# Four banks for attention, a three-step weight decode and ScalarE softmax steps in the first twelve slots of a fused attention and feed-forward kernel

## The chip, the cores and the metric

The kernel runs on one core of a Trainium2 chip. The metric is the device time of one execution in microseconds (us), and the median of several runs is quoted. Five engines work side by side, each through its own queue in order: PE (TensorE, matmuls), DVE (VectorE), ACT (ScalarE), POOL (GpSimd) and SP (SyncE, which here issues every DMA). An instruction that waits holds up everything behind it on its engine.

## What is computed

Attention over keys and values that are mean-pooled by eight, then two feed-forward layers, all in float32. Shapes: batch 8, 8 heads, 576 tokens, head size 64, so 72 pooled keys a head; then 4608 tokens by 512, with 2048 hidden units in each layer.

```python
def _attn_ref(q, k, v):
    k_p = k.reshape(B, H, Sp, pool, D).mean(axis=3)      # 576 keys -> 72
    v_p = v.reshape(B, H, Sp, pool, D).mean(axis=3)
    scores = scale * np.matmul(q, k_p.transpose(0, 1, 3, 2))
    scores = scores - np.max(scores, axis=-1, keepdims=True)
    attn = np.exp(scores)
    attn = attn / (np.sum(attn, axis=-1, keepdims=True) + 1e-09)
    return np.matmul(attn, v_p)

def _moe_ref(x, w_in, w_out):
    h = x @ w_in
    return (h * np.clip(h + 3.0, 0.0, 6.0) / 6.0) @ w_out

def _moe2_ref(x, w_in, w_out, a, b):
    h = x @ w_in
    P = a[0] + a[1] * h + a[2] * h**2 + a[3] * h**3
    Q = 1.0 + np.abs(b[0]) * np.abs(h) + np.abs(b[1]) * h**2
    return (P / (Q + 1e-6)) @ w_out
```

## The kernel before

Every large product is made from two parts of each operand: a rounded high part and the remainder as a low part, both in a faster float32 form. High by high, high by low and low by high give three matmuls per block. So each weight chunk and each activation is split by ScalarE (the rounding copy) and VectorE or GpSimd (the subtraction).

**Slots.** The program is a list of slots, written out in order by `slot(s)`. Nothing reorders it afterwards. Slots -12 to -1 (`PRE = 12`) are a start-up; from slot 0 on, each slot of layer 1 holds one hidden block (`hidden`, line 448, twelve matmuls into `ps_h`) and one output block of two slots ago (`out1`, line 473, into `ps_y`). Layer 1 has 9 token blocks of 16 slots, then layer 2 has as many. What a slot holds besides is put into lists by kind (`el`, `pe`, `ex`, `nz`, `mid`, `hi`, `la`, and `dm` and `ld` for loads), and `slot` goes through these lists in a fixed order, the same before slot 0 as after.

**Attention.** A unit is 128 (or fewer) query tokens for four heads. Its steps are: `scores` (line 334, PE), `highest` (the maximum, line 349, and its scaling, line 350, both DVE), `exponentials` (line 359, four ACT instructions that also give the sums), `normalize` (line 368 adds 1e-9 to the sums and line 370 takes the reciprocal, both DVE; lines 371 and 377 multiply on POOL), `transposes` (line 386, three on PE), `split_p` (line 397 on ACT, lines 398 and 402 on DVE). After the units of one half of the heads, `attend` (line 415, eight matmuls) multiplies by the values, and `split_x` (lines 426 and 427) makes the layer's input. The transposes of unit i and the scores of unit i+2 stand in one slot, the exponentials and the normalizing of unit i+1 in the same slot. In slots -10 to -1 stand the transposes t0 to t3, an attend (slot -6), t4 to t7, and an attend (slot -1): ten slots for eight units and two attends. Scores, transposes and attends take turns on two PSUM banks, `a0` and `a1`:

```python
    def bank_a(name):
        turn[0] ^= 1
        return ps_a.tile([P, 512], F32, tag=f"a{turn[0]}", name=name)
```

**The first values.** For batch 0 the pooling of the values is done on PE: `pool_first_v` (line 279) makes eight small matmuls per chunk, six chunks in all, three in slot -11 and three in slot -10. `split_v` (line 293 on ACT, 294 on DVE), `mask_v` (line 303, POOL) and `mask_rest` (lines 314 to 319, DVE) make the operands of the attend from them, in slots -10 and -9.

**Weights.** Layer 1 has 32 chunks of 128x512. They come as raw 64-bit words and are turned into float32 by `decode_a` and `decode_r` (lines 153 and 158, ACT), `decode_b` (lines 172 and 173, DVE) and `decode_c` (line 180, POOL), then split by `split_weights` (line 200 ACT, 202 DVE or POOL). In the start-up, chunk i is decoded in slot i-12 and split one slot later (chunks 10 and 11 both in slot -2, chunk 12 in slot -1), all by `make_ready`, which stands in the list `el`: behind the exponentials of the slot and ahead of its normalizing, its `split_p` and its maximum.

Of the kernel before, what the change touches and what calls it, by code (L numbers as in the profile page):

```python
# [68 lines left out]
def feed_forward_kernel(tc, q_t, k_t, v_r, vmask, w_in1, w_out1, w_in2, w_out2, a_rep, b_rep, out):  # L69
# [25 lines left out]
    def consts():  # L95
# [8 lines left out]
        nc.gpsimd.memset(cst[:, 1:2], (1.0 + 1e-6) * 2.0 ** -LN_SHIFT)  # L104
        nc.gpsimd.memset(cst[:, 2:3], -LN_SHIFT * math.log(2.0))
        nc.vector.tensor_scalar(
            out=coef[:, 6:10], in0=coef[:, 0:4], scalar1=-1.0, scalar2=None, op0=ALU.mult
# [41 lines left out]
    def decode_a(*c):  # L149
        hi = raw[c].bitcast(I32).rearrange("p (n t) -> p n t", t=2)[:, :, 1].bitcast(F32)  # L150

        dec[c] = ps_h.tile([P, DM], F32, tag="h", name="d") if c[0] == 0 and 2 * c[1] + c[2] < PRE else hi
        nc.scalar.activation(out=dec[c], in_=hi, func=AF.Copy, scale=2.0 ** -112)
# [170 lines left out]

    def bank_a(name):
        turn[0] ^= 1
        return ps_a.tile([P, 512], F32, tag=f"a{turn[0]}", name=name)

    def scores(b, g, f, ti):
        _, n = ti  # L330
        ps = bank_a("ps_s")
        q = q_sb.pop((b, f, ti))
        for i in range(2):
            nc.tensor.matmul(  # L334
                ps[:n, i * 2 * SP:(i + 1) * 2 * SP],
                lhsT=q[:, i, :n],
                rhs=kbd[:, 2 * f + i].rearrange("p j s -> p (j s)"),
                start=True,
                stop=True,
            )  # L340
        sc_ps[b, f, ti] = ps
# [3 lines left out]
    def highest(b, f, ti):  # L345
# [3 lines left out]
        nc.vector.tensor_reduce(out=nm[:n], in_=ps, axis=AX.X, op=ALU.max, negate=True)  # L349
        nc.vector.tensor_scalar(out=nm[:n], in0=nm[:n], scalar1=SCALE, scalar2=None, op0=ALU.mult)  # L350

    def exponentials(b, f, ti):
        _, n = ti
        ps, nm = sc_ps.pop((b, f, ti)), s_max.pop((b, f, ti))
        s = s_sb[b, f, ti] = att.tile([P, 2 * PK + P], F32, tag="s", bufs=2, name="s")
        sm = s_sum[b, f, ti] = att.tile([P, 4], F32, tag="sm", bufs=2, name="sm")
        for h in range(4):
            c = slice(h * SP, (h + 1) * SP)
            nc.scalar.activation(  # L359
                out=s[:n, c], in_=ps[:n, c], func=AF.Exp, scale=SCALE, bias=nm[:n, h:h + 1], accum_out=sm[:n, h:h + 1]  # L360
            )

    def normalize(b, f, ti):
# [3 lines left out]
        sm = s_sum.pop((b, f, ti))  # L367
        nc.vector.tensor_scalar(out=sm[:n], in0=sm[:n], scalar1=1e-9, scalar2=None, op0=ALU.add)
        rc = att.tile([P, 4], F32, tag="rc", bufs=2, name="rc")
# [11 lines left out]
    def transposes(b, g, f, ti):  # L381
        _, n = ti
        s = s_sb.pop((b, f, ti))
        ps = bank_a("ps_t")
        for c, o in enumerate((0, PK, 2 * PK)):
# [20 lines left out]
    def attend(b, g, f, i):  # L406
        n = GROUPS[b][g][1]
        ph, pl = pth[b, g, f], ptl[b, g, f]
        ps = bank_a("ps_v")
        wh, wl, wr = (  # L410
# [156 lines left out]

    pe, ex, el, nz, mid, hi, la, dm, ld = {}, {}, {}, {}, {}, {}, {}, {}, {}

# [7 lines left out]
    def prepare_first(s0, units):  # L577
# [9 lines left out]
        for c in range(VCH):  # L587
            at(dm, s0, load_v, 0, c)
            at(pe, s0 + 1 + c // 3, pool_first_v, c)
        at(dm, s0, load_weights, 0, *chunks[1])  # L590
        for p in (0, NPAIR, 1):
            at(el, s0, pool_first_k, p)
        for p in (2, 3):
            at(el, s0 + 1, pool_first_k, p)
        at(la, s0 + 2, split_v, 0)
        for i in range(4):
            at(la, s0 + 3 + i // 2, mask_v, 0, i // 2, i % 2)
        at(la, s0 + 3, mask_rest, 0)

# [72 lines left out]
    for i in range(len(chunks) + 1):  # L672
        s = i - PRE if i < 10 else 3 * (i - 10) // 4 - 2
        if 2 <= i < len(chunks):
            at(dm if i < 24 else ld, s - 2, load_weights, 0, *chunks[i])
# [40 lines left out]
    def slot(s):  # L716
        d = s - LAG
        for f in dm.get(s, ()):
            f()
# [105 lines left out]
```

## Time and profile before

| what | us |
|---|---|
| median of 3 runs | 1797.69 |
| lowest and highest of them | 1795.35 and 1800.09 |
| the profiled execution | 1796.08 |
| its span in the profile | 1794.3 |
| PE busy | 1733.5 (97%) |
| DVE busy | 1019.1 (57%) |
| ACT busy | 955.5 (53%) |
| POOL busy | 915.0 (51%) |

PE works nearly all the time over the whole span, and the other engines about half of it. Those shares are means over stages that differ much, so they say little about the first twelve slots, which end where the first matmul into `ps_h` starts, 93.26 us into the span. How to read the views: a timeline row has the start, the time of the row, the engine, the line, the operation, what is written and read, and in brackets how long the engine had been idle and what ended that. Where a row stands for several instructions, its time is that of all of them. A wait is put down to what came last.

### The profile page before, as it was taken

To read this page: it belongs to the slowest core of one execution; us is meant where nothing else is said; L and a number is where in the kernel's file an instruction comes from. 1 tells how busy PE (TensorE), PEld (TensorE's weight loads), DVE (VectorE), ACT (ScalarE), POOL (GpSimd) and SP (SyncE) were. 2 spreads that over 40 slices of the span, in tenths; PEclk is the share of its full clock that TensorE was granted. 3 is DMA by queue.
4 is the path that set the end of the run, shared out by engine and by line. 5 is a ranking of instruction groups with operands and counts; after the bars stand their busy time and mean duration, and the time that the engine had idled before them with its cause. 6 is when DMAs were issued, how large, how long until landed. Compare 5 with 4: busy or idle time off the path is not lost.

```text
span 1794.3 us, 22345 instructions
## 1 busy us (share of the span) xinstructions
PE 1733.5 (97%) x7872; PEld 1433.5 (80%) x7872; DVE 1019.1 (57%) x1771; ACT 955.5 (53%) x2072; POOL 915.0 (51%) x887
## 2 busy tenths in 40 slices
PE   7388999999999999999999999999999999999999
PEld 6276788888888888888888888888888888888887
DVE  4786544646455463643311466666666666666665
ACT  3565444554444454544322466666666666666665
POOL 2556433343434343343323476667666666666665
PEclk9589999999999999999999999999999999999999
DMA  5352122314142242422026401010101010101000
GB/s 175 117 184 83 44 81 67 130 64 161 57 136 91 75 149 64 135 81 80 30 95 220 143 18 36 12 36 13 36 12 41 7 42 6 42 6 42 1 24 24
DMA packets 68336, 128.33 MB, mean 72 GB/s; under 512 B 11392, under 2 KB 27776, under 8 KB 68224
## 3 DMA queue, kind: packets, MB, share of 16 engines
q1 hardware_dynamic: 68224, 126.91, 21.3%
q8 instruction: 62, 1.02, 0.2%
q14 instruction: 50, 0.41, 0.1%
HBM read 91.23 MB, written 35.65 MB: 71 GB/s over the span
## 4 chain that ended last, share of the span: by engine, by line
PE 87%; DVE 1%; ACT 0%; DMA 0%; POOL 0%; issue 0%; SPq 0%; ACTq 0%; DVEq 0%
PE ps_h L448 41%; PE ps_o L553 22%; PE ps_y L473 20%; PE ps_s L334 2%; PE ps_v L415 2%; PE ps_t L386 1%; DMA v_raw<-v_r 0%; ACT s L359 0%; DVE t L173 0%; POOL gl L462 0%; POOL gl L539 0%; ACT y L479 0%; DVE vsum L247 0%; DVE t L172 0%; DVE nm L349 0%
## 5 line engine op out<-in xcount | busy, mean ns | idle before, releaser
L462 POOL TENSOR_TENSOR gl<-r,gh 128x512 fp32r<-128x512 f32 x144 | 187.5, 1302 | 478.5 <-ACT gh L461 474.8
L473 PE MATMUL ps_y<-gh,w 128*128 128x512 f32 x1152 | 391.8, 401 | 0.0
L448 PE MATMUL ps_h<-xh,w 128*128 128x512 f32 x1152 | 379.4, 390 | 0.5 <-DVE r L455 0.5
L448 PE MATMUL ps_h<-x2h,w 128*128 128x512 f32 x1152 | 377.8, 389 | 0.8 <-DVE t L515 0.8
L553 PE MATMUL ps_o<-w,gh 128*128 128x512 f32 x1152 | 354.6, 389 | 0.0
L473 PEld LDWEIGHTS ps_y<-gh,w 128*128 128x128 f32 x1152 | 219.2, 190 | 47.3 <-issue 1.8
L448 PEld LDWEIGHTS ps_h<-xh,w 128*128 128x128 f32 x1152 | 216.8, 188 | 46.2 <-DVE r L455 0.9
L448 PEld LDWEIGHTS ps_h<-x2h,w 128*128 128x128 f32 x1152 | 216.4, 188 | 46.2 <-DVE t L515 1.2
L553 PEld LDWEIGHTS ps_o<-w,gh 128*128 128x128 f32 x1152 | 216.3, 188 | 45.0
L510 POOL TENSOR_SCALAR qd<-ah,coef 128x512 f32<-128x512 f32 x144 | 111.4, 773 | 234.0 <-ACT ah L508 234.0
L473 PE MATMUL ps_y<-gl,w 128*128 128x512 f32 x576 | 226.9, 394 | 0.0
L448 PE MATMUL ps_h<-xl,w 128*128 128x512 f32 x576 | 224.5, 390 | 0.0
L523 DVE SCALAR_TENSOR_TENSOR qd<-qd,r 128x512 f32<-128x512 f32 x144 | 99.0, 688 | 220.5 <-ACT r L522 204.0
L448 PE MATMUL ps_h<-x2l,w 128*128 128x512 f32 x576 | 224.1, 389 | 0.0
L553 PE MATMUL ps_o<-w,gl 128*128 128x512 f32 x576 | 224.1, 389 | 0.0
L539 POOL TENSOR_TENSOR gl<-g,gh 128x512 fp32r<-128x512 f32 x144 | 186.5, 1295 | 19.3 <-ACT gh L538 19.3
L513 POOL TENSOR_TENSOR qd<-qd,ah 128x512 f32<-128x512 f32 x144 | 187.1, 1300 | 12.1
L455 DVE SCALAR_TENSOR_TENSOR r<-r,ps_h 128x512 f32<-128x512 f32 x144 | 98.2, 682 | 149.1 <-ACT r L454 148.6
L508 ACT ACTIVATE ah<-ps_h 128x512 f32<-128x512 f32 x144 | 86.1, 598 | 151.9 <-PE ps_h L448 151.9
L521 ACT ACTIVATE r<-qd,cst 128x512 f32<-128x512 f32 x144 | 99.6, 692 | 105.4 <-POOL qd L513 105.4
L461 ACT ACTIVATE gh<-r 128x512 fp32r<-128x512 f32 x144 | 91.3, 634 | 118.7 <-PE ps_y L473 109.2
L359 ACT ACTIVATE s<-ps_s,nm 128x72 f32<-128x72 f32 (+1 forms) x320 | 98.2, 318 | 91.6 <-DVE nm L350 84.8
(89 smaller groups left out, 2608.2 us busy)
## 6 DMA issues: line engine op xcount, KB each, us to landing
raw<-w_in SPq DMA_DIRECT2D x32, 512.0 KB, 3.7
raw<-w_out SPq DMA_DIRECT2D x32, 512.0 KB, 3.8
w<-raw SPq DMA_DIRECT2D x32, 512.0 KB, 2.9
w<-w SPq DMA_DIRECT2D x32, 512.0 KB, 4.1
v_raw<-v_r SPq DMA_DIRECT2D x47, 256.0 KB, 4.0
y<-y SPq DMA_DIRECT2D x36, 256.0 KB, 2.9
x2r<-y SPq DMA_DIRECT2D x36, 256.0 KB, 2.9
out<-o SPq DMA_DIRECT2D x36, 256.0 KB, 2.2
```

What stands on the lines that cost most here:

```text
L359: nc.scalar.activation(out=s[:n, c], in_=ps[:n, c], func=AF.Exp, scale=SCALE, bias=nm[:n, h:h + 1], accum_out=sm[:n, h:h + 1])
L448: nc.tensor.matmul(ps, lhsT=w, rhs=x, start=o == 0, stop=o == len(ops) - 1)
L455: nc.vector.scalar_tensor_tensor(out=r, in0=r, scalar=1.0, in1=ps, op0=ALU.min, op1=ALU.mult)
L461: nc.scalar.activation(out=gh[it], in_=r, func=AF.Copy)
L462: nc.gpsimd.tensor_tensor(out=gl[it], in0=r, in1=gh[it].bitcast(F32), op=ALU.subtract)
L473: nc.tensor.matmul(yp[j][c], lhsT=w, rhs=x, start=m == 0 and o == 0, stop=m == MF - 1 and o == 2)
L510: nc.gpsimd.tensor_scalar(out=qd, in0=ah, scalar1=absb[1], scalar2=absb[0], op0=ALU.mult, op1=ALU.add)
L513: nc.gpsimd.tensor_tensor(out=qd, in0=qd, in1=ah, op=ALU.mult)
L521: nc.scalar.activation(out=r0, in_=qd, func=AF.Ln, scale=2.0 ** -LN_SHIFT, bias=cst[:, 1:2])
L523: nc.vector.scalar_tensor_tensor(out=qd, in0=qd, scalar=1.0 + 1e-6, in1=r0, op0=ALU.add, op1=ALU.mult)
L539: nc.gpsimd.tensor_tensor(out=gl[it], in0=g, in1=gh[it].bitcast(F32), op=ALU.subtract)
L553: nc.tensor.matmul(yp[j][c], lhsT=w, rhs=x, start=m == 0 and o == 0, stop=m == MF - 1 and o == 2)
```

## The change

There are four edits.

- **Banks.** For batch 0's first group (`b + g == 0`) scores, transposes and attends go round four banks: `a0`, `y2`, `a1`, `y3`. The two `y` banks belong to `out1`, which first uses them in slot 2. Later units still alternate between `a0` and `a1`.
- **The order within slots -12 to -1.** These slots get an order of their own: loads, the early `el`, `pe`, the maximum (`hi`), exponentials, normalizing, the middle step of a weight chunk (`c1`), `mid`, the split of the chunk before (`c2`), the first step of the chunk after (`c3`), `la`. The decode of a chunk thus spreads over three slots. Chunks 0 to 10 go this way (before, chunks 0 to 12 were begun by slot -1); from chunk 11 on, three chunks are made ready in two slots, where it was four in three. Both ways reach chunk 24 in slot 8, and chunk 31 in slot 13.
- **Values.** One chunk is summed in slot -11, two in slot -10, two in slot -9, one in slot -8. Splitting and masking move with them by two slots, to slots -8, -7 and -6.
- **Small softmax steps.** The scaling of the maximum and the adding of 1e-9 become ACT instructions on 128x4 elements, in `exponentials`, for all 80 units. DVE loses both.

```diff
-        dec[c] = ps_h.tile([P, DM], F32, tag="h", name="d") if c[0] == 0 and 2 * c[1] + c[2] < PRE else hi
+        dec[c] = ps_h.tile([P, DM], F32, tag="h", name="d") if c[0] == 0 and 2 * c[1] + c[2] < PRE - 1 else hi
...
-    def bank_a(name):
-        turn[0] ^= 1
+    def bank_a(name, first):
+
+        if first:
+            turn[0] = (turn[0] + 1) % 4
+            pool, tag = ((ps_a, "a0"), (ps_y, "y2"), (ps_a, "a1"), (ps_y, "y3"))[turn[0]]
+            return pool.tile([P, 512], F32, tag=tag, name=name)
+        turn[0] = turn[0] % 2 ^ 1
         return ps_a.tile([P, 512], F32, tag=f"a{turn[0]}", name=name)
...
         nc.vector.tensor_reduce(out=nm[:n], in_=ps, axis=AX.X, op=ALU.max, negate=True)
-        nc.vector.tensor_scalar(out=nm[:n], in0=nm[:n], scalar1=SCALE, scalar2=None, op0=ALU.mult)
...
+        nc.scalar.activation(out=nm[:n], in_=nm[:n], func=AF.Copy, scale=SCALE)
         for h in range(4):
...
+        nc.scalar.activation(out=sm[:n], in_=sm[:n], func=AF.Identity, bias=cst[:n, 3:4])
...
-        nc.vector.tensor_scalar(out=sm[:n], in0=sm[:n], scalar1=1e-9, scalar2=None, op0=ALU.add)
...
-            at(pe, s0 + 1 + c // 3, pool_first_v, c)
+            at(pe, s0 + 1 + (c + 1) // 2, pool_first_v, c)
...
-        at(la, s0 + 2, split_v, 0)
+        at(la, s0 + 4, split_v, 0)
         for i in range(4):
-            at(la, s0 + 3 + i // 2, mask_v, 0, i // 2, i % 2)
-        at(la, s0 + 3, mask_rest, 0)
+            at(la, s0 + 5 + i // 2, mask_v, 0, i // 2, i % 2)
+        at(la, s0 + 5, mask_rest, 0)
...
     for i in range(len(chunks) + 1):
-        s = i - PRE if i < 10 else 3 * (i - 10) // 4 - 2
-        if 2 <= i < len(chunks):
+        if i < PRE - 1:
+
+            s, c = i + 1 - PRE, (0, *chunks[i])
+            if i > 1:
+                at(dm, max(s - 3, -PRE), load_weights, *c)
+            at(c3, s - 1, decode_a, *c)
+            at(c3, s - 1, decode_r, *c)
+            at(c1, s, decode_b, *c)
+            at(c1, s, decode_c, *c)
+            if i < PRE - 2:
+                at(c2, s + 1, split_weights, *c)
+            continue
+        s = 2 * (i + 1 - PRE) // 3
+        if i < len(chunks):
             at(dm if i < 24 else ld, s - 2, load_weights, 0, *chunks[i])
         at(el, s, make_ready, i)
...
         d = s - LAG
+        if s < 0:
+            for kind in (dm, ld, el, pe, hi, ex, nz, c1, mid, c2, c3, la):
+                for f in kind.get(s, ()):
+                    f()
+            return
```

On PE the instructions of the first slots stand in this order before (`ps_k` pools the keys, `ps_s` are scores, `ps_vs` the sums of the values, `ps_t` the transposes; x8, x16 and x24 are one, two and three chunks of values).

```order
L334 MATMUL ps_s<-kbd,q_sb 128x144 x2
L279 MATMUL ps_vs<-k_raw,ident 128x64 x8
L279 MATMUL ps_vs<-v_raw,ident 128x64 x16
L386 MATMUL ps_t<-ident,s 128x128 x3
L334 MATMUL ps_s<-kbd,q_sb 128x144 x2
L279 MATMUL ps_vs<-v_raw,ident 128x64 x24
L386 MATMUL ps_t<-ident,s 128x128 x3
L334 MATMUL ps_s<-kbd,q_sb 128x144 x2
```

And after, in the same stretch of PE, up to the fourth set of transposes:

```order
L340 MATMUL ps_s<-kbd,q_sb 128x144 x2
L280 MATMUL ps_vs<-k_raw,ident 128x64 x8
L392 MATMUL ps_t<-ident,s 128x128 x3
L340 MATMUL ps_s<-kbd,q_sb 128x144 x2
L280 MATMUL ps_vs<-v_raw,ident 128x64 x16
L392 MATMUL ps_t<-ident,s 128x128 x3
L340 MATMUL ps_s<-kbd,q_sb 128x144 x2
L280 MATMUL ps_vs<-v_raw,ident 128x64 x16
L392 MATMUL ps_t<-ident,s 128x128 x3
L340 MATMUL ps_s<-kbd,q_sb 128x144 x2
L280 MATMUL ps_vs<-v_raw,ident 128x64 x8
L392 MATMUL ps_t<-ident,s 128x128 x3
```

The first transposes stand behind one chunk of values instead of three, and the other chunks are spread behind the next three units. From there on PE's order is the same in both kernels.

On DVE one start-up slot reads like this before (`t<-d` and `t<-d,t` are decode_b, `w` is the split, `sm` and `rc` belong to normalizing, `ptl` and `pth` to split_p, `nm` to the maximum).

```order
L172 TENSOR_SCALAR t<-d 128x512
L173 SCALAR_TENSOR_TENSOR t<-d,t 128x512
L202 TENSOR_TENSOR w<-t,w 128x512
L368 TENSOR_SCALAR sm<-sm 128x4
L370 RECIPROCAL rc<-sm 128x4
L398 TENSOR_TENSOR ptl<-ps_t,pth 128x2x128
L402 TENSOR_TENSOR pth<-ps_t,pth 32x128
L349 TENSOR_REDUCE nm<-ps_s 128x4
L350 TENSOR_SCALAR nm<-nm 128x4
```

And one start-up slot of DVE after:

```order
L355 TENSOR_REDUCE nm<-ps_s 128x4
L376 RECIPROCAL rc<-sm 128x4
L173 TENSOR_SCALAR t<-d 128x512
L174 SCALAR_TENSOR_TENSOR t<-d,t 128x512
L404 TENSOR_TENSOR ptl<-ps_t,pth 128x2x128
L408 TENSOR_TENSOR pth<-ps_t,pth 32x128
L203 TENSOR_TENSOR w<-t,w 128x512
```

The maximum has moved from the end of the slot to its head, the reciprocal ahead of the decode, and `sm` and the second `nm` are gone.

On ACT one start-up slot after has its two new rows (lines 362 and 368) around the exponentials, and the decode's first step behind everything else:

```order
L362 ACTIVATE nm<-nm 128x4
L365 ACTIVATE s,sm<-ps_s,nm 128x72 x4
L368 ACTIVATE sm<-sm,cst 128x4
L403 ACTIVATE pth<-ps_t 128x3x128
L201 ACTIVATE w<-t 128x512
L154 ACTIVATE d<-raw_260 128x512
L159 ACTIVATE raw_260<-raw_260 128x512
```

Before, lines 153, 158 and 200 stood between the exponentials and the copy into `pth`; now they stand behind it. SP's order is unchanged up to the load of chunk 10: the loads of keys, values, queries and these chunks stand where they stood.

## Rows read from the trace of the kernel before

**Rows 1.** Windows: us, busy us (instructions) of PE, PEld, DVE, ACT, POOL; clock, DMA, GB/s.

```profile
0.00:93.26 93.26, 52.20 (x224) 44.52 (x225) 54.90 (x107) 41.69 (x138) 34.04 (x48) 0.74 0.43 143
93.26:225.00 131.74, 117.23 (x516) 93.92 (x515) 94.78 (x173) 74.38 (x204) 74.30 (x71) 0.93 0.32 104
225.00:900.00 675.00, 674.11 (x3212) 558.81 (x3211) 330.06 (x731) 317.18 (x915) 257.46 (x282) 1.00 0.28 93
```

**Rows 2.** PE's three longest waits, 38 to 93.2 us: total, times, longest.

```profile
PE ps_v L415 <- DVE pth L402: 8.8, 2, 5.7
PE ps_t L386 <- POOL s L377: 8.7, 2, 4.4
PE ps_t L386 <- DVE nm L350: 7.6, 2, 4.0
```

**Rows 3.** Timeline of PE: values, transposes and attends of the start-up, first hidden block.

```profile
24.18 7.03 PE L279 MATMUL ps_vs<-v_raw,ident 128*128 128x64 f32 x32
31.01 0.85 PE L386 MATMUL ps_t<-ident,s 128*128 128x128 f32 x3
...
32.61 6.02 PE L279 MATMUL ps_vs<-v_raw,ident 128*128 128x64 f32 x48
...
52.82 0.90 PE L386 MATMUL ps_t<-ident,s 128*128 128x128 f32 x3 [4.38 <-POOL s L377]
...
57.82 0.76 PE L415 MATMUL ps_v<-pth,vh 128*128 128x512 f32 x1 [3.14 <-DVE pth L402]
...
89.36 0.77 PE L415 MATMUL ps_v<-pth,vh 128*128 128x512 f32 x1 [5.68 <-DVE pth L402]
...
93.26 0.63 PE L448 MATMUL ps_h<-xh,w 128*128 128x512 f32 x1
```

**Rows 4.** Timeline of PE: transposes, then scores, then `ps_y`, later at full clock.

```profile
125.09 0.49 PE L386 MATMUL ps_t<-ident,s 128*128 128x128 f32 x3
...
125.82 0.48 PE L473 MATMUL ps_y<-gh,w 128*128 128x512 f32 x1
```

**Rows 5.** Timeline of ACT in slot -7: exponentials, decode, split, split_p.

```profile
51.80 0.32 ACT L359 ACTIVATE s<-ps_s,nm 128x72 f32<-128x72 f32 x1 [2.75 <-DVE nm L350]
...
53.00 0.64 ACT L153 ACTIVATE d<-raw 128x512 f32<-128x512 f32 x1
...
54.63 0.49 ACT L397 ACTIVATE pth<-ps_t 128x384 fp32r<-128x384 f32 x1
```

**Rows 6.** Timeline of DVE in slot -7: decode, reciprocal, split_p, maximum.

```profile
53.68 0.69 DVE L172 TENSOR_SCALAR t<-d 128x512 int32<-128x512 int32 x1 [1.99 <-ACT d L153]
...
56.89 0.18 DVE L370 RECIPROCAL rc<-sm 128x4 f32<-128x4 f32 x1
56.98 0.39 DVE L398 TENSOR_TENSOR ptl<-ps_t,pth 128x256 fp32r<-128x256 f32 x1
...
57.70 0.46 DVE L349 TENSOR_REDUCE nm<-ps_s 128x4 f32<-128x288 f32 x1
```

**Rows 7.** Timeline of POOL, slots -8 and -7: decode_c, masks, normalizing.

```profile
49.16 1.28 POOL L180 TENSOR_TENSOR t<-t,raw 128x512 int32<-128x512 int32 x1 [2.42 <-ACT pth L397]
...
52.72 0.61 POOL L303 TENSOR_TENSOR vh<-vsh,mask 128x256 fp32r<-128x256 f32 x1
...
57.21 0.40 POOL L371 TENSOR_TENSOR s<-s,rc 128x128 f32<-128x128 f32 x1 [0.38 <-DVE rc L370]
57.69 0.67 POOL L377 TENSOR_TENSOR s<-s,rc 128x288 f32<-128x288 f32 x1
```

**Rows 8.** Groups by line and shape, 0 to 93.3 us: count, busy us, mean ns, idle.

```profile
L368 DVE TENSOR_SCALAR sm<-sm 128x4 f32<-128x4 f32 x8 | 7.8, 976 | 0.0
...
L109 ACT ACTIVATE coef<-coef 128x2 f32<-128x2 f32 x1 | 0.2, 203 | 1.4 <-DMA coef<-b_rep 1.4
```

**Rows 9.** Timeline of POOL and PE in a later slot of layer 1.

```profile
404.06 1.29 POOL L462 TENSOR_TENSOR gl<-r,gh 128x512 fp32r<-128x512 f32 x1 [4.11 <-ACT gh L461]
...
407.26 0.39 PE L473 MATMUL ps_y<-gl,w 128*128 128x512 f32 x1
```

More of the change, by code (lines that the diff above doesn't have):

```diff
@@ L105, in consts @@
         nc.gpsimd.memset(cst[:, 2:3], -LN_SHIFT * math.log(2.0))
+        nc.gpsimd.memset(cst[:, 3:4], 1e-9)
         nc.vector.tensor_scalar(
@@ L330, in scores @@
         _, n = ti
-        ps = bank_a("ps_s")
+        ps = bank_a("ps_s", b + g == 0)
         q = q_sb.pop((b, f, ti))
@@ L383, in transposes @@
         s = s_sb.pop((b, f, ti))
-        ps = bank_a("ps_t")
+        ps = bank_a("ps_t", b + g == 0)
         for c, o in enumerate((0, PK, 2 * PK)):
@@ L408, in attend @@
         ph, pl = pth[b, g, f], ptl[b, g, f]
-        ps = bank_a("ps_v")
+        ps = bank_a("ps_v", b + g == 0)
         wh, wl, wr = (
@@ L565, in evac2 @@
             nc.sync.dma_start(out=out[r:r + P, :], in_=o)
-    pe, ex, el, nz, mid, hi, la, dm, ld = {}, {}, {}, {}, {}, {}, {}, {}, {}
+    pe, ex, el, nz, mid, hi, la, dm, ld, c1, c2, c3 = ({} for _ in range(12))
     def at(kind, slot, f, *a):
```

## The prediction

> **What bounds the kernel now.** I read the windows first, because they say where a change to the start-up can count at all. From 225 to 900 us PE is busy for 674.11 of 675.00 us [rows 1]: there only PE's own work sets the time, and this change leaves that work as it is. Up to 93.26 us PE is busy for 52.20 us, and from there to 225 us for 117.23 of 131.74 us. So 41 us of PE time stand idle before the first hidden block and 14.5 us in the stretch behind it. Whatever brings the first hidden block forward shortens the run by as much, as long as the stretch behind it doesn't hand it back.
>
> The timeline splits the start-up in two. Up to the end of the values PE is full: two chunks take 24.18 to 31.01, then t0 and the next scores until 32.61, then three chunks in 6.02 us [rows 3]. After that the slots wait for a round trip. PE's longest waits are for DVE's `pth` and `nm` and POOL's `s` [rows 2], the ends of each slot's chain: exponentials on ACT, decode and reciprocal on DVE, normalizing on POOL, then DVE's split_p and maximum, from which ACT's next exponentials start. ACT stood idle 2.75 us for `nm` at 51.80, while DVE's decode of 53.68 had waited for ACT [rows 5, 6]. The two take turns, and each slot pays for both in a row.
>
> **The change part by part.** I replay the start-up with durations of rows, PE's marks first. Transposes and scores of a slot take 32.61 - 31.01 = 1.60 us here and 125.82 - 125.09 = 0.73 us later at the higher clock [rows 3, 4]. A chunk of values takes 6.83 / 2 = 3.4 us in the first pair and 6.02 / 3 = 2.0 us in the last three.
>
> *Values.* t0 stands behind one chunk instead of three, so it comes two chunks sooner: 31.0 - 6.8 = 24.2. The other five chunks now lie between the units, and PE is the bound: t0 and scores 1.6, two chunks 6.8 (32.6), t1 and scores 0.73, two chunks 4.0 (37.3), t2 and scores 0.73, the last chunk 2.0: 40.1 for t3. The loop must keep up. Behind the scores that end at 38.1, the maximum takes 0.46, the reciprocal's hand-over to POOL 0.32 (56.89 to 57.21) and normalizing 1.15 (57.21 to 58.36) [rows 6, 7]: 40.0, just in time. So t3 starts at 40.1 instead of 52.82 [rows 3]: 12.7 us won.
>
> *Masks, the part that costs.* They come two slots later and now the first attend waits for them. The high part of the sums takes ACT 0.5 (as the copy at 54.63), to 40.6; `nm`, exponentials (51.80 to 53.00, 1.2) and `sm` 1.6, to 42.2; hand-over and normalizing 1.5, to 43.7 [rows 5, 7]. Then POOL has a decode_c and a split, which with one normalizing took 52.72 - 49.16 = 3.56, so 2.4 without it, to 46.1, and two masks of 0.6 each [rows 7]. The attend's first matmul can go at 46.7 and its third at 47.3; I take 47.0. Before, it was 57.82: 10.8 of the 12.7 are left.
>
> *The four banks and the new order,* slots -6 to -1. An attend lasts 93.26 - 89.36 = 3.9 [rows 3], to 50.9; ACT stands behind it with its copy of the result. t4, t5 and their scores no longer wait, since their inputs were normalized slots earlier and their banks are free. ACT then has one copy of 0.5, twice the group decode and split (53.00 to 54.63, 1.63) and one `pth` of 0.5: 55.2. The softmax of unit 6 takes 1.6, hand-over and normalizing 1.5: t6 at 58.3. For t7, ACT goes on from 56.8 with `pth` 0.5, decode and split 1.63 and unit 7's exponentials with `nm` 1.4, to 60.3. The scores of unit 8 are the first that go back to two banks, and wait for those exponentials: 1.0 for them (1.60 less 0.6 of transposes) and 0.46 for the maximum give 61.8, and behind it on DVE stand the reciprocal 0.1, the decode 2 x 0.69 and split_p 0.72 (56.98 to 57.70) [rows 6]: t7, whose bank split_p frees, at 64.0. Once more with unit 9's scores behind t7 (0.6 + 1.0) and its maximum, 66.1, and the same 2.2 on DVE: the second attend at 68.3 instead of 89.36, the first hidden block at 72.2 instead of 93.26 [rows 3]. That is 21 us. The replay leaves out the small gaps between engines; I take 2 us off for these, an estimate of 4% of the 48 us behind t0. **19 us** remain. The ends: nothing at all if the slots keep their old pace, and 41 us if PE never waited [rows 1].
>
> *Small steps.* In these slots DVE's `sm` took 976 ns on average over 8, far more than the reciprocal's 180 ns; POOL was at its decode_c beside it. An ACT instruction on two columns took 203 ns [rows 8]. I take 0.2 each for the two steps that move. The bounds are 0.1 (hidden in part behind the one ahead) and 0.32, what a 72-column exponential takes [rows 5]: with eight units, 2 us either way, inside the range.
>
> The Trainium skill speaks against this part: its page ScalarE: Activation LUTs, section Rules for kernel authors, puts multiplications and additions on VectorE; by the figures there an ACTIVATE of four columns with a pointer bias would take about 280 ns, an estimate which makes the sum less than 1 us worse. In these slots the trace disagrees with the rule: DVE's 976 ns is the dearer one.
>
> *Slots from 0 on.* DVE loses both steps for the units in the idle stretch up to 225 us, some dozen, and there two more chunks are to be decoded and split, 2 x (2 x 0.69 + 0.7) = 4.2 us of DVE. DVE's 94.78 us of 131.74 [rows 1] become lighter by some 8 us. PE's 14.5 idle us there may shrink or, where two chunks fall into one slot more often, grow. I take 1 us won, with -5 and +4 as ends. In the rest of layer 1, 70 units carry two more ACT steps; 1.9 us lie between POOL's end of `gl` (404.06 + 1.29) and its use at 407.26 [rows 9], so 0.4 us are covered, and without that cover would cost up to 70 x 0.4 = 28 us. Loads keep their order on SP; 143 GB/s [rows 1] become 143 x 93.26 / 72 = 185 for the same bytes, and each load still stands two slots ahead of its use.
>
> Sum against the profiled execution: 1796.08 - 19 - 1 = 1776.1. The median of the runs lies 1.6 above that execution: 1777.7, so **1778 us**.
>
> **The rivals.**
>
> *The slots stay long.* The values' 12.7 us come, the masks take 1.9 back, and behind the first attend the slots keep their old 31.5 us (57.82 to 89.36) because ACT and DVE are still in series, the last two units on two banks: 1797.7 - 10.8 = 1787. For it: five of the waits above pass through ACT, which is held by each attend. Against it: DVE's maximum now goes to the head of the slot, and ACT's idle 2.75 us [rows 5] were the wait for it.
>
> *PE keeps its higher clock.* The granted clock averages 0.74 before 93.26 us [rows 1]. If the tighter slots hold it high, transposes and scores of t0 and t4 to t7 cost 0.87 less each, 4 us, the first two chunks 2.8, the attends about 3.5 together: 10 us more, 1768. Against it: PE would still wait for about a third of slots -7 to -1.
>
> *Slower.* The two steps on ACT cost what `sm` costs on DVE. Then `gh` behind them in each later unit comes late, `gl` too, and PE waits at `ps_y` (line 473). It decides from the 1.9 us of cover [rows 9]: with 1.1 us per step, (2.2 - 1.9) x 70 = 21 us eat the whole gain; at 1.25 per step it is (2.5 - 1.9) x 70 - 20 = +22: 1820. Against it: 203 ns [rows 8]. The skill's rule above is this rival's rule, though its figure is far below that point.
>
> *No change.* The idle time moves behind the first hidden block: the weights or keys of slots 0 to 8 are late on DVE, which is busy 94.78 of 131.74 us there [rows 1], and PE waits there for what it saved: 1797.
>
> **How the numbers follow.** Forecast 0.64, slots stay long 0.20, higher clock 0.08, no change 0.05, slower 0.03. The range goes from 1768, the higher clock, to 1789, which takes in the long slots with 2 us of ACT steps at the upper bound; what is left out is the last two cases and a little of the edges. A measurement of this kernel can tell about 0.3% (5 us) from no change: faster 0.92, same 0.05, slower 0.03.
>
> **What would show it.** t0 near 24, t3 near 40, the first attend near 47 with POOL's masks as its releaser, the first hidden block near 72; no `nm` wait of PE's transposes; ACT's two steps at about 0.2 us; PE full again from about 205. The forecast is wrong if the slots behind the first attend take over 5.5 us, or if PE's idle time behind the first hidden block grows beyond 19 us.

## The result, and the profile after

The changed kernel takes 1776.84 us (median of four runs, 1774.42 to 1780.08), and the kernel before, beside it, 1798.89: a ratio of 0.988 with a 95% interval of 0.986 to 0.991. The profiled execution took 1774.73 us with a span of 1772.9. I call the two kernels "before" and "after".

The first part of the page of after gives busy time, share and instructions:

```profile
PE 1726.1 (97%) x7872; PEld 1429.6 (81%) x7872; DVE 984.0 (56%) x1611; ACT 992.5 (56%) x2232; POOL 911.1 (51%) x888
```

DVE lost 35 us and ACT gained 37, as the small steps moved over; neither bounds the whole. The windows say where the time went (columns as in [rows 1]). They end at the first hidden block, at the point where PE has become full, and inside layer 1:

```profile
0.00:68.59 68.59, 44.15 (x224) 39.65 (x225) 41.64 (x81) 42.53 (x151) 29.48 (x48) 0.81 0.52 176
68.59:203.15 134.56, 117.52 (x515) 94.32 (x513) 95.30 (x156) 83.01 (x231) 77.05 (x72) 0.92 0.34 111
203.15:878.00 674.85, 673.87 (x3211) 558.67 (x3211) 306.94 (x613) 344.97 (x1034) 256.07 (x283) 1.00 0.28 93
```

The start-up fell from 93.26 us to 68.59, and PE's idle time in it from 41.1 to 24.4 us. The stretch behind it became longer: the same work of PE (515 and 516 matmul records) now stands in 134.56 us instead of 131.74, with 17.0 us idle instead of 14.5. The third row is as before [rows 1]: 1 us idle in 675. The clock column counts time for which the trace holds no clock record as 1.00, so the 0.81 here and the 0.74 of [rows 1] are too high (see the last section). On PE's timeline the marks of the forecast read:

```profile
24.75 3.91 PE L280 MATMUL ps_vs<-v_raw,ident 128*128 128x64 f32 x32
...
35.75 0.55 PE L392 MATMUL ps_t<-ident,s 128*128 128x128 f32 x3 [0.19 <-POOL s L383]
...
43.03 0.80 PE L421 MATMUL ps_v<-pth,vh 128*128 128x512 f32 x1 [6.24 <-POOL vh L304]
...
65.04 0.77 PE L421 MATMUL ps_v<-pth,vh 128*128 128x512 f32 x1 [2.77 <-ACT sm L368]
...
68.59 0.63 PE L454 MATMUL ps_h<-xh,w 128*128 128x512 f32 x1
...
233.87 0.48 PE L479 MATMUL ps_y<-gh,w 128*128 128x512 f32 x1
```

The last row is the first matmul of the 21st output block. I use it as a mark behind the stretch in which PE still waits. In before it stands at 255.41:

```profile
255.41 0.48 PE L473 MATMUL ps_y<-gh,w 128*128 128x512 f32 x1
```

From it to the end of the span lie 1539.0 us in after and 1538.9 in before, and between 1538.0 and 1539.3 in every kernel below. So all that differs lies ahead of the mark, and the 57 units behind it (80 less ten in the start-up and thirteen from there to the mark) carry their two more ACT steps for nothing.

PE's waits from 30 us to the first hidden block (total, times, longest) are no longer those of [rows 2]:

```profile
PE ps_v L421 <- POOL vh L304: 6.2, 1, 6.2
PE ps_t L392 <- DVE t L174: 4.8, 1, 4.8
PE ps_v L421 <- ACT sm L368: 2.8, 1, 2.8
PE ps_t L392 <- DVE pth L408: 2.6, 1, 2.6
```

No transposes wait for `nm` any more. The longest wait is the new one, for POOL's masks.

The times of one kernel fall into two groups: after's ten runs gave 1774.0 to 1775.6 or 1778.9 to 1783.5, and before's 1794.8 to 1796.4 or 1797.7 to 1801.4. One difference between executions can be seen in the traces: PE's first pair of value chunks took 3.9 us in the profile above and 6.9 in others, because PE's clock rose later there (last section). So between kernels I compare stretches that begin behind that pair, and give its length:

| kernel | median us | ratio to before (95%) | first value pair | t3 | first hidden block H | t3 to H | H to mark |
|---|---|---|---|---|---|---|---|
| before (first profile) | 1797.69 | | 7.0 | 52.8 | 93.3 | 40.4 | 162.1 |
| b_again | 1795.83 (one run) | | 7.0 | 52.5 | 93.0 | 40.4 | 162.2 |
| after | 1776.84 | 0.988 (0.986 to 0.991) | 3.9 | 35.8 | 68.6 | 32.8 | 165.3 |
| a2_again | 1779.49 | 0.989 (0.987 to 0.991) | 6.9 | 40.7 | 73.2 | 32.5 | 165.9 |
| u1_small | 1782.22 | 0.991 (0.989 to 0.994) | 6.9 | 41.0 | 74.0 | 33.0 | 168.8 |
| u2_banks | 1780.96 | 0.990 (0.989 to 0.992) | 6.9 | 41.7 | 75.1 | 33.4 | 166.9 |
| u3_values | 1786.49 | 0.993 (0.991 to 0.996) | 7.0 | 51.1 | 80.3 | 29.2 | 165.3 |
| u4_order | 1780.95 | 0.990 (0.988 to 0.993) | 6.9 | 44.2 | 81.2 | 37.0 | 159.3 |
| p2_pace | 1778.50 | 0.989 (0.987 to 0.990) | 6.9 | 40.9 | 73.7 | 32.8 | 165.0 |
| m1_masks | 1774.98 | 0.988 (0.986 to 0.989) | 3.9 | 37.2 | 68.7 | 31.5 | 165.4 |
| c1_both | 1775.95 | 0.987 (0.985 to 0.989) | 4.3 | 36.7 | 67.9 | 31.2 | 163.3 |
| o1_more | 1774.63 | 0.987 (0.985 to 0.990) | 6.9 | 40.8 | 74.5 | 33.7 | 159.1 |
| o2_early | 1772.77 | 0.986 (0.983 to 0.989) | 6.9 | 41.1 | 72.9 | 31.8 | 160.6 |

### The profile page after: what moved, and what is told of

Same layout as the page of the kernel before. It is cut to its first block, busy times and chain, and to the rows that moved or that the text cites. A ratio compares the mean times of both kernels' runs of the same rounds, so it can differ in the third digit from the quotient of the medians.

```text
span 1772.9 us, 22385 instructions
## 1 busy us (share of the span) xinstructions
PE 1726.1 (97%) x7872; PEld 1429.6 (81%) x7872; DVE 984.0 (56%) x1611; ACT 992.5 (56%) x2232; POOL 911.1 (51%) x888
## 4 chain that ended last, share of the span: by engine, by line
PE 89%; ACT 1%; DVE 0%; POOL 0%; DMA 0%; issue 0%; SPq 0%; DVEq 0%
PE ps_h L454 41%; PE ps_o L559 22%; PE ps_y L479 20%; PE ps_s L340 2%; PE ps_v L421 2%; PE ps_t L392 1%; DMA v_raw<-v_r 0%; ACT s L365 0%; POOL gl L468 0%; POOL gl L545 0%; ACT r L460 0%; POOL t L181 0%; ACT y L485 0%; DVE vsum L248 0%; DVE t L521 0%
## 5 line engine op out<-in xcount | busy, mean ns | idle before, releaser
L460 ACT ACTIVATE r<-ps_h,cst 128x512 f32<-128x512 f32 x144 | 98.5, 684 | 84.0 <-PE ps_h L454 76.4
```

Of the source, the lines that this page charges most:

```text
L460: nc.scalar.activation(out=r, in_=ps, func=AF.Relu, bias=cst[:, 0:1], scale=1.0 / 6.0)
```

## The experiments

The theory: the start-up is shorter because t0 stands behind one value chunk, because the order and the banks take PE out of the round trip between ACT and DVE, and what follows the first hidden block is worth little. The rivals are that one of the four edits does it all, or that a stretch behind hands the gain back. The first four kernels each undo one edit of after.

### u1_small: the small steps back on DVE

```diff
+        nc.vector.tensor_scalar(out=nm[:n], in0=nm[:n], scalar1=SCALE, scalar2=None, op0=ALU.mult)
...
-        nc.scalar.activation(out=nm[:n], in_=nm[:n], func=AF.Copy, scale=SCALE)
...
-        nc.scalar.activation(out=sm[:n], in_=sm[:n], func=AF.Identity, bias=cst[:n, 3:4])
...
+        nc.vector.tensor_scalar(out=sm[:n], in0=sm[:n], scalar1=1e-9, scalar2=None, op0=ALU.add)
```

> The changed kernel with only the two small softmax steps back on DVE (scaling of the maximum behind the maximum, the 1e-9 ahead of the reciprocal), for all units. Theory (the steps on DVE lie in the start-up's chain, and the one ahead of the reciprocal is stretched to about 1 us by POOL's decode_c): eight slots get up to 1 us longer where the chain sets them, and DVE, busy 92 of 131 us behind the first hidden block, carries some 10 us more: the first hidden block 2 to 5 us later than 68.6, the run 2 to 6 us above 1776.8. Rival (where these steps run makes no difference, since PE waits for other things): within 1.5 us, first hidden block at 68 to 70. Rival (the steps are dearer on ScalarE): faster by 1 to 3 us.

Measured: 1782.22 us. The start-up barely moves (H at 74.0, against 73.2 in a2_again); the stretch behind it takes 168.8 us instead of 165.9, up to the mark at 242.83:

```profile
242.83 0.49 PE L479 MATMUL ps_y<-gh,w 128*128 128x512 f32 x1
```

The groups by line and shape of after, 0 to 73 us (count, busy us, mean ns, idle before):

```profile
L368 ACT ACTIVATE sm<-sm,cst 128x4 f32<-128x4 f32 x8 | 2.4, 298 | 0.3
L362 ACT ACTIVATE nm<-nm 128x4 f32<-128x4 f32 x8 | 1.6, 197 | 0.0
```

The same view of u1_small, same window:

```profile
L374 DVE TENSOR_SCALAR sm<-sm 128x4 f32<-128x4 f32 x8 | 1.7, 216 | 0.1
L356 DVE TENSOR_SCALAR nm<-nm 128x4 f32<-128x4 f32 x8 | 1.4, 170 | 0.3
```

In the new order DVE is the cheaper engine for `sm` in the start-up: 216 ns, where it took 976 on average before [rows 8]. So the other three edits had already made `sm` short there without moving it: it now stands ahead of POOL's decode and not beside it. Behind the first hidden block it stands beside that decode again in part of the units, and takes 655 ns on average over nine, as two rows of DVE's timeline in u1_small show:

```profile
103.88 0.16 DVE L374 TENSOR_SCALAR sm<-sm 128x4 f32<-128x4 f32 x1
...
119.29 1.27 DVE L374 TENSOR_SCALAR sm<-sm 128x4 f32<-128x4 f32 x1
```

and POOL's beside them:

```profile
101.65 1.30 POOL L468 TENSOR_TENSOR gl<-r,gh 128x512 fp32r<-128x512 f32 x1 [2.13 <-ACT gh L467]
104.09 1.30 POOL L181 TENSOR_TENSOR t<-t,raw 128x512 int32<-128x512 int32 x1 [1.14 <-ACT r L460]
...
118.90 1.63 POOL L181 TENSOR_TENSOR t<-t,raw 128x512 int32<-128x512 int32 x1 [1.15 <-ACT pth L403]
```

With POOL idle, from 102.95 to 104.09, `sm` takes 0.16 us. Where it starts inside POOL's decode it takes 1.27 us and ends with it, at 120.56 against 120.53. The Trainium skill (page Advanced Engine Details and Errata, section Mode Summary) says that VectorE's second SBUF port is shared with GpSimd, and that GpSimd's instructions and VectorE's two-port ones block each other; these rows agree with it, though no run shows that `sm` is a two-port instruction. The price is ACT's, which stands behind in the chain. ACT's longest wait from 73.5 to 212 us in u1_small:

```profile
ACT s L365 <- DVE nm L356: 23.5, 11, 3.5
```

and in a2_again:

```profile
ACT nm L362 <- DVE nm L355: 16.3, 11, 2.8
```

What follows: the two ACT steps gain 3.7 us at the mark, 2.9 of them behind the first hidden block, and not for the reason that I gave.

### u2_banks: two banks everywhere

```diff
-        if first:
+        if False:
```

> The changed kernel with two banks (a0, a1) for all units, as before; the rest as changed. Theory (with two banks a slot's scores wait for the exponentials of the same slot, as the slots -3 and -2 of the changed kernel show: 5.8 us and 4.8 us from transposes to transposes or attend): the slots from the second unit on take 5 to 6 us, t3 comes at 41 to 44 instead of 35.8, the first hidden block 5 to 9 us later, the run 1782 to 1786. Rival (the new order alone brings the gain, the banks were never what a slot waited for): first hidden block within 1.5 us of 68.6.

Measured: 1780.96 us; t3 1.0 and H 1.9 us later than in a2_again, the mark 2.8 later. PE's waits from 30 to 75 us:

```profile
PE ps_t L392 <- DVE pth L408: 8.8, 4, 2.7
PE ps_v L421 <- POOL vh L304: 5.1, 1, 5.1
```

Four transposes, not one, now wait for split_p to free their bank, 8.8 us instead of 2.6. But the wait of t6 (5.4 us in a2_again) is gone in exchange, and the wait for the masks is 5.1 us instead of 6.3. H is 6.5 us behind the 68.6 that I had started from, but a2_again is 4.6 behind it too, and the run is below the 1782 to 1786 that I expected. What follows: the banks are worth 2 to 3 us, a small part.

### u3_values: the values and masks in their old slots

```diff
-            at(pe, s0 + 1 + (c + 1) // 2, pool_first_v, c)
+            at(pe, s0 + 1 + c // 3, pool_first_v, c)
...
-        at(la, s0 + 4, split_v, 0)
+        at(la, s0 + 2, split_v, 0)
...
-            at(la, s0 + 5 + i // 2, mask_v, 0, i // 2, i % 2)
-        at(la, s0 + 5, mask_rest, 0)
+            at(la, s0 + 3 + i // 2, mask_v, 0, i // 2, i % 2)
+        at(la, s0 + 3, mask_rest, 0)
```

> The changed kernel with the six chunks of values in two slots and their splitting and masking in slots -10 to -8, as before. Theory (the first transposes stand behind three chunks, then the loop of about 4 us a slot is free of the masks): t0 at 29 to 31 instead of 23.2, t3 at 41 to 43 instead of 35.8, but the attend follows t3 by 5 us instead of 7.3: first hidden block 3 to 5 us later, run 1780 to 1782. Rival (the masks' wait takes back all that the values won): within 1.5 us. Rival (the full gain of 7 us hangs on the values): 6 to 8 us later.

Measured: 1786.49 us, the slowest of the four; its interval begins where after's ends. H is at 80.3. On PE's timeline of u3_values:

```profile
31.81 10.34 PE L280 MATMUL ps_vs<-v_raw,ident 128*128 128x64 f32 x48
41.94 0.85 PE L392 MATMUL ps_t<-ident,s 128*128 128x128 f32 x3
...
80.33 0.63 PE L454 MATMUL ps_h<-xh,w 128*128 128x512 f32 x1
```

t1 stands behind six chunks at 41.9 where in a2_again it starts at 31.8; of these ten us seven remain at H; the wait for the masks ahead of the first attend, which after has in exchange, isn't there in u3_values. I had expected H 3 to 5 us later and a run of 1780 to 1782; 7.1 us at H fit the last rival (6 to 8). But part of it is PE's clock: the three chunks took 10.34 us here and 6.02 in before [rows 3], since the clock rose at 58.35 us in this execution and at 33.8 in before's (last section). Up to 4.3 of the 7.1 us may come from that. What follows: by the medians (7.0 and 9.7 us above after's two) and at the mark (6.5 us later) the values are the largest single edit; what they are worth at the same clock was not measured.

### u4_order: the old order within slots -12 to -1, with the old weight decode

```diff
-        s = 2 * (i + 1 - PRE) // 3
-        if i < len(chunks):
+        s = i - PRE if i < 10 else 3 * (i - 10) // 4 - 2
+        if 2 <= i < len(chunks):
...
-        if s < 0:
+        if False:
```

(The branch of three steps for chunks 0 to 10 is taken out with it, so chunks 0 to 12 are decoded in the start-up again.)

> The changed kernel with the slots -12 to -1 in the order of before (decode and split in one list between exponentials and normalizing, maximum last) and the pace of the weight chunks of before; four banks, spread values and small steps on ScalarE stay. Theory (the order is what takes ACT and DVE out of series): slots of 5.5 to 6.5 us again, first hidden block 10 to 15 us later than 68.6, and the stretch behind it 3 us shorter than in the changed kernel since the chunks have the old pace: the run 1784 to 1789. Rival (banks, values and small steps bring most of it without the order): first hidden block 0 to 5 us later, run 1774 to 1779.

Measured: 1780.95 us. H is 8.0 us later than in a2_again, at 81.2, but the mark only 1.4:

```profile
240.50 0.48 PE L479 MATMUL ps_y<-gh,w 128*128 128x512 f32 x1
```

I had expected 3 us back behind H and a run of 1784 to 1789. PE's longest wait from 30 to 81.2 us:

```profile
PE ps_t L392 <- POOL s L383: 14.3, 4, 9.5
```

and the window behind H:

```profile
81.20:209.77 128.57, 116.17 (x514) 92.92 (x513) 88.06 (x151) 80.17 (x226) 74.72 (x71) 0.93 0.33 108
```

Against a2_again's window (below), which holds the same 514 matmul records, it is 6.6 us shorter: PE idles 12.4 us instead of 16.3, and is busy for 2.7 us less, at a mean granted clock of 0.93 instead of 0.91. DVE is lighter by 5.9. What follows: the order brings 8 us, and 6.6 of them are handed back behind the first hidden block, where after has two chunks more to decode (o1_more checks that it is these and not the order). This is the cost that the prediction had small.

### a2_again: after, unaltered

> The changed kernel once more, unaltered. In its first profile the pair of value chunks behind the first transposes took 3.9 us, in the profiles of the kernel before and of four variants 6.9 to 7.0. Theory (the pair's pace differs from execution to execution and the first profile was an early one): the pair takes 6.9 us here, t1 comes near 31.5 and the first hidden block near 71.5. Rival (the changed kernel as such gets PE up to speed earlier): the pair again 3.9 us, first hidden block within 1 us of 68.6. The median within 0.2% of 1776.8 either way.

Measured: 1779.49 us over six runs. PE's timeline of a2_again:

```profile
25.04 6.93 PE L280 MATMUL ps_vs<-v_raw,ident 128*128 128x64 f32 x32
...
40.70 0.55 PE L392 MATMUL ps_t<-ident,s 128*128 128x128 f32 x3 [0.19 <-POOL s L383]
...
48.00 0.79 PE L421 MATMUL ps_v<-pth,vh 128*128 128x512 f32 x1 [6.25 <-POOL vh L304]
...
70.00 0.77 PE L421 MATMUL ps_v<-pth,vh 128*128 128x512 f32 x1 [2.77 <-ACT sm L368]
...
73.23 0.39 PE L454 MATMUL ps_h<-xh,w 128*128 128x512 f32 x1
...
239.14 0.48 PE L479 MATMUL ps_y<-gh,w 128*128 128x512 f32 x1
```

and its window behind H:

```profile
73.23:208.41 135.18, 118.86 (x514) 95.28 (x513) 93.94 (x157) 83.13 (x231) 77.61 (x73) 0.91 0.34 111
```

Against the first profile of after, nearly all that differs is PE's pace up to 35.3 us, in the first value pair and the beginning of the next: t3 comes 4.95 us later, H 4.64, the mark 5.27, the end 5.5. What follows: two executions of the same program differ by this, and a forecast from rows of the slower pace is to be held against this profile.

### p2_pace: chunks from 11 on spread 10 over 7 slots

```diff
-        s = 2 * (i + 1 - PRE) // 3
+        s = (7 * (i + 1 - PRE) + 5) // 10
```

> The changed kernel with another pace of the weight chunks from chunk 11 on: ten chunks in seven slots, one chunk in slot 0 (before: four in three with two chunks more done by slot 0; changed: three in two, with two chunks in slot 0). Chunk 31 comes in slot 14 instead of 13. Theory (the stretch behind the first hidden block lost 3.3 us in the changed kernel, mostly in slots 0 to 5, because two chunks fall into every second slot and split_p waits behind them): the first hidden block stays, the distance from it to the steady part shrinks by 2 to 5 us, run 1772 to 1775. Rival (the loss comes from the tighter start-up as such, loads and keys being late): no change, 1775.5 to 1778.

Measured: 1778.50 us, H to mark 165.0 instead of 165.9. What follows: that two chunks fall into one slot every other time is not where the 6.6 us go; the theory of the pace falls, but for about 1 us.

### m1_masks: the masks ahead of the chunk's middle step, in slot -7 alone

```diff
-            for kind in (dm, ld, el, pe, hi, ex, nz, c1, mid, c2, c3, la):
+            for kind in (dm, ld, el, pe, hi, ex, nz, *((la, c1) if s == 5 - PRE else (c1,)), mid, c2, c3, *((la,) if s != 5 - PRE else ())):
```

> The changed kernel with split values masked in slot -7 ahead of that slot's weight chunk on POOL and DVE (la ahead of c1 in that slot alone). Theory (the first attend waits 6.2 us for POOL's masks, which stand behind a decode_c and a split of 1.28 and 1.26 us; DVE's four steps of the rest stand behind decode and split_p): the attend comes 2 to 2.5 us sooner after t3 (5 us instead of 7.3), the slots behind it follow, first hidden block 1.5 to 2.5 us sooner, run about 1775. Rival (ACT, whose chunks stand behind the attend, sets the pace of what follows anyway): the attend sooner, the first hidden block the same within 0.7 us.

The wait of 6.2 us ahead of the first attend is explained by POOL's timeline in after:

```profile
39.15 0.67 POOL L383 TENSOR_TENSOR s<-s,rc 128x288 f32<-128x288 f32 x1
39.91 1.28 POOL L181 TENSOR_TENSOR t<-t,raw 128x512 int32<-128x512 int32 x1
41.15 1.26 POOL L203 TENSOR_TENSOR w<-t,w 128x512 fp32r<-128x512 f32 x1
42.37 0.61 POOL L304 TENSOR_TENSOR vh<-vsh,mask 128x256 fp32r<-128x256 f32 x1
```

The decode and a split stand ahead of the mask, 2.5 us that PE waits for. Measured: 1774.98 us; on PE's timeline of m1_masks:

```profile
41.85 0.79 PE L421 MATMUL ps_v<-pth,vh 128*128 128x512 f32 x1 [3.66 <-POOL vh L304]
43.59 0.79 PE L421 MATMUL ps_v<-ptl,vh 128*128 128x512 f32 x1 [0.95 <-DVE ptl L404]
```

The attend starts 4.7 us behind t3 instead of 7.3, but its second matmul waits for `ptl`, and H comes only 1.0 to 1.3 us sooner behind t3 (31.5 against 32.5 and 32.8). That lies between what I expected and what the rival gave (under 0.7): most of the 2.5 us turned into later waits.

### c1_both: m1_masks and p2_pace together

> Both: the masks ahead of the chunk in slot -7, and the pace of ten chunks in seven slots. Theory (the two waits lie in different stretches and add): 3 to 6 us below the changed kernel, 1771 to 1774. Rival (what one wins, the other's stretch hands back): as the better of the two alone.

Measured: 1775.95 us, with t3 to H 31.2 and H to mark 163.3. The profiled execution, at 1771.16, was the fastest of its four. By its median it is no faster than m1_masks alone, and above the 1771 to 1774 that I expected. What follows: by the marks the pace gives 2.1 us here and gave 0.9 alone, so 1 to 2; the medians don't show it.

### b_again: before, unaltered

> The kernel before once more, for its trace alone. The times of both kernels fall into two groups some 5 us apart (before: 1795 to 1796 and 1800 to 1801). Theory (the groups are two paces of PE's first 32 us, as in the changed kernel, whose two profiles are 5.5 us of span apart and differ by 4.6 us up to the first hidden block): if this execution is of the other group, the pair of value chunks takes about 3.9 us instead of 7.0, or the first hidden block is about 5 us away from 93.3. Rival (the groups come from somewhere else): the first hidden block within 1.5 us of 93.3 whatever the time.

Measured: 1795.83 us, with t3, H and the mark within 0.3 us of the first profile. It is an execution of the same kind as that one, so this run decides nothing between theory and rival.

### o1_more: m1_masks, and chunks 11 and 12 decoded in the start-up

```diff
+    MID = [*range(1 - PRE, -5), -5, -5, -4, -3, -2, -1, -1]
...
-        if i < PRE - 1:
+        if i < len(MID):
...
-            s, c = i + 1 - PRE, (0, *chunks[i])
+            s, c = MID[i], (0, *chunks[i])
...
-        s = 2 * (i + 1 - PRE) // 3
+        s = 3 * (i - 10) // 4 - 2
```

(With this the new order within the slots stays, two slots hold two chunks, and the pace behind is that of before.)

> The changed kernel with the masks ahead of the chunk in slot -7, and with chunks 11 and 12 decoded in the start-up too (two chunks in slot -5 and two in slot -1), so that the pace from chunk 13 on is that of before. Theory (decoding is work of ACT, DVE and POOL that is only moved: the start-up got rid of two chunks, and the stretch behind pays 6 us for them, 165.9 instead of 159.3 us from the first hidden block to a mark in token block 2 with the order of before): the start-up 3 to 6 us longer than with the masks alone, the stretch behind 4 to 7 us shorter, the run within 2 us of 1775. Rival (the stretch behind is long because of the pace of three in two, and the start-up has room for two more chunks): start-up within 1.5 us, run 1768 to 1771.

Measured: 1774.63 us. The window behind H:

```profile
74.50:202.93 128.43, 114.95 (x514) 91.94 (x513) 91.41 (x154) 80.60 (x226) 75.98 (x71) 0.94 0.34 108
```

H to mark is 159.1, within 0.2 us of u4_order, though the order within the start-up is another. The start-up pays 2.2 us (t3 to H 33.7 against m1's 31.5), less than the 3 to 6 that I expected. What follows: the two chunks and the pace that goes with them, not the order, are the 6.6 us.

### o2_early: m1_masks, and one chunk more at the very start

```diff
+        at(dm, s0, load_weights, 0, *chunks[1])
         for c in range(VCH):
...
-        if i < PRE - 1:
+        if i < PRE:
...
-            s, c = i + 1 - PRE, (0, *chunks[i])
+            s, c = max(i, 1) - PRE, (0, *chunks[i])
...
-        s = 2 * (i + 1 - PRE) // 3
+        s = 3 * (i - PRE) // 4
```

> The changed kernel with the masks ahead of the chunk in slot -7, and with chunk 1 loaded ahead of the values and decoded together with chunk 0 in slot -12, where ACT and DVE stand idle from 12.5 to 19.5 us; each later chunk of the start-up is one slot sooner, chunk 11 too lies in it, and four chunks in three slots follow. Theory (idle time of ACT pays for one chunk): start-up within 1 us of that with the masks alone, the stretch behind 2.5 to 4 us shorter, run 1770 to 1773. Rival (512 KB ahead of the values make PE wait for them): PE waits for the values, the start-up 1.5 to 3 us longer, run 1774 to 1777.

Measured: 1772.77 us, the lowest median of all kernels here, with a ratio to before of 0.986 (0.983 to 0.989). The window behind H:

```profile
72.90:202.81 129.91, 115.02 (x514) 92.60 (x513) 91.77 (x154) 81.18 (x228) 76.67 (x71) 0.93 0.35 111
```

Chunk 1 is loaded ahead of the values and decoded with chunk 0. ACT's timeline of o2_early shows the place that it takes:

```profile
13.69 0.64 ACT L154 ACTIVATE d<-raw 128x512 f32<-128x512 f32 x1 [1.55 <-DMA raw<-w_out]
14.26 0.65 ACT L159 ACTIVATE raw<-raw 128x512 int32<-128x512 uint32 x1
15.56 0.45 ACT L274 ACTIVATE kbd<-ps_k 64x64 f32<-64x64 f32 x2 [0.66 <-PE ps_k L273]
```

In a2_again ACT stands idle there, for the keys:

```profile
15.10 0.45 ACT L274 ACTIVATE kbd<-ps_k 64x64 f32<-64x64 f32 x2 [3.05 <-PE ps_k L273]
```

The start-up pays 0.3 us (31.8 against 31.5), and the stretch behind it gains 4.8 (160.6 against 165.4), more than the 2.5 to 4 that I expected. At the same first value pair its mark is 5.6 us ahead of a2_again's. By the runs alone its interval overlaps after's; against before the whole interval lies below 1.

## Why the prediction was right, and which step of it was not

**The time.** 1776.84 us against 1778: the forecast case came in, with two errors of opposite sign inside it.

**Values, t0 and t3: right.** t0 at 23.2 to 23.4 (24.2 forecast), and t3 at 40.7 (40.1) where the first value pair ran at the pace of [rows 3]. By u3_values this edit carries the most at the mark, with the clock's part of it open.

**Masks: right in kind and size.** The first attend stood at 48.0 (47.0) behind POOL's `vh`, with the decode and the split ahead of it as worked out. m1_masks shows that the order of three POOL instructions decides there.

**Slots -6 to -1: right.** t4 and t5 do not wait. t6 waits for POOL's normalized `s`, as worked out (59.4 against 58.3). The wait list names DVE's `t`, which PE doesn't read; in after it ends 0.01 us behind `s`, and there PE's weight load for the same transposes names POOL:

```profile
54.41 0.29 PEld L392 LDWEIGHTS ps_t<-ident,s 128*128 128x128 f32 x2 [4.99 <-POOL s L383]
```

t7 waits for `pth` (65.2 against 64.0), and the second attend came at 70.0 (68.3) and H at 73.2 (72.2). The allowance of 2 us for gaps held half. u2_banks and u4_order share the gain: 1.9 us by the banks and 8.0 by the order.

**Small steps: the reason was wrong, the sign right.** I took 0.2 us for each ACT step, and `nm` took 0.197 but `sm`, whose bias comes from a tile, 0.298. For such a bias the Trainium skill (ScalarE: Activation LUTs, section What ACT_TABLE_LOAD costs) gives about 280 ns ahead of the columns, and the 298 ns agree with it. I also wrote that DVE's 976 ns is the dearer one; u1_small shows 216 ns for it in the new start-up. The step that failed was to take a time that came from POOL's decode beside it for a property of the instruction. Behind the first hidden block `sm` is long again on DVE, and there the move pays.

**Slots from 0 on: the term that was mis-sized.** I took 1 us won, with -5 and +4 as ends. H to mark grew by 3.1 us in the first profile and by 3.8 in a2_again. The parts close: small steps on ACT win 2.9 (u1_small's 168.8 against 165.9; u4_order against before, which differ there by the small steps, 159.3 against 162.1 and 162.2, gives about the same), and two chunks fewer in the start-up, with their pace, cost 6.6 (159.3 against 165.9): 6.6 - 2.9 = 3.7. I had priced both by DVE's busy time: 4.2 us for the chunks, outweighed by some 8 us that DVE gets lighter. In the runs the chunks outweigh the steps. The pattern of the pace is the smaller part of the 6.6 (1 to 2 us, by p2_pace and c1_both), and the two chunks are not alike: o2_early gets 4.8 us back with one of them, and its own pace. Of the 6.6, 3.9 are more idle time of PE and 2.7 more busy time, at a lower mean clock (u4_order). DVE itself is 5.9 us busier there, so my 4.2 was low even as DVE's price. That the idle part comes from a chunk's way through ACT, DVE, POOL, ACT and DVE again, each in order, is argued and not shown by a run of its own.

**What made it look better than it was.** The first profile of after had the quick value pair, and that was luck: 24.7 us won up to H, 5.7 more than the forecast's 19, which covers the 4.1 us by which the stretch behind H missed its forecast. In a2_again both errors stand open: 1796.08 - 20.0 (start-up) + 3.8 (stretch) gives 1779.9, and that execution took 1780.16, 4 us above the 1776.1 forecast for it.

**The rivals.** "The slots stay long" did not come: from the first attend to the second it took 22.0 us instead of 31.5. "Slower" did not come: behind the mark nothing differs, though `sm` takes 0.1 us more than taken. "No change" named the right mechanism, time that moves behind the first hidden block, and was too large: 3.8 us of 20. "PE keeps its higher clock" did not come in the slots that I named: from 52.5 us to the first hidden block after's clock records hold 0.50, the level of 1.2 GHz. What came is an earlier first rise in some executions (25.2 us in after's first profile, against 33.8 in before and 35.3 in a2_again, whose 20 us thus don't come from it). The 0.74 that this rival started from is a misreading: with the 33.8 us that have no record at the lower level it is about 0.56, an estimate from the records and PE's pace.

Left open: why u1 to u4 at the mark add up to 3.7 + 2.8 + 6.5 + 1.4 = 14.4 us, and the whole change, from before to a2_again, is 16.3, since no run undid two of them and u3_values ran at another clock.

## What to carry to other kernels

Work that is moved out of a start-up into a stretch where PE still waits is priced by what PE loses there: here 6.6 us for two chunks with their pace, where a sum over the fullest engine's busy time had given a small gain. Before an instruction is moved away from an engine where it looks dear, look at what runs beside it: a 4-column VectorE step took 0.16 us with GpSimd idle and 1.27 us beside GpSimd's decode, and in the new start-up, where it no longer stands beside it, 0.22 us on average. And where an engine stands idle at the very start (o2_early), one more chunk there is nearly free.

## What the hardware showed beyond this

The clock column of the windows reads 1.00 in the first part of every profile, and PE's pace does not agree: there the trace holds no clock record, and the column counts such time as full. In after the list of clock records begins at 25.21 us, with the level of 2.4 GHz. The 2 us ahead of this and behind it (us, PE busy, clock, DMA share, GB/s):

```profile
23.21:25.21 2.00, 2.00 (x11) 1.00 0.12 41
25.21:27.21 2.00, 2.00 (x20) 1.00 0.55 154
```

In a2_again the list begins at 35.27 us:

```profile
33.27:35.27 2.00, 2.00 (x12) 1.00 0.32 72
35.27:37.27 2.00, 2.00 (x20) 1.00 0.78 253
```

PE is busy throughout in all four, and runs 11 or 12 instructions ahead of the first record and 20 behind it; in before, whose list begins at 33.76 us, it is 11 and 20. So PE worked at the pace of the lower level (1.2 GHz) until then. The same 32 small matmuls took 6.93 us in a2_again, where they lie ahead of the rise, and 3.91 us in after, where nearly all lie behind it.

The first record stands at 26.6 us in m1_masks and c1_both, at 33.8 in b_again, at 58.35 in u3_values and at 34.4 to 36.7 in the others. What makes the clock rise sooner in one execution than in another was not found: after and a2_again are the same program, and PE was busy without a gap from 16 us on in both. Between these two it is worth 4.6 us at the first hidden block and 5.5 us of the span. From a time alone it can't be told, since o1_more and o2_early had profiles of 1773 to 1774 us with the slow pair.
